# 18 heads with a column of ones in V, one float32 product that turns and folds a head's result, divisions on VectorE, and a new order of the plan

## The chip, the cores and the metric

The kernel runs on one core of one Trainium2 chip. The metric is the device time of one execution in microseconds (us), as the median of the runs shown. Engines are called as the profile calls them: PE is TensorE (PEld its weight loads), DVE is VectorE, ACT is ScalarE, POOL is GpSimd, SP issues the transfers.

## The reference: what is computed

Pooled attention over 4 batches of 8 heads, 1152 keys of 64 numbers each, queries averaged in pairs (576 of them), then a token mixer and a channel mixer. All inputs and the output are float32 (the mixers' weights arrive as float64).

```python
q_pool = q.reshape(B, H, S // 2, 2, D).mean(axis=3)          # B, H, S, D = 4, 8, 1152, 64
scores = scale * np.matmul(q_pool, k.transpose(0, 1, 3, 2))
scores = scores - np.max(scores, axis=-1, keepdims=True)
attn = np.exp(scores)
attn = attn / (np.sum(attn, axis=-1, keepdims=True) + 1e-09)
x = np.matmul(attn, v)                                       # then heads side by side: (4, 576, 512)
xt = x.transpose(0, 2, 1)
u = x + (np.maximum(xt @ w_tok1, 0.0) @ w_tok2).transpose(0, 2, 1)
out = u + np.maximum(u @ w_ch1, 0.0) @ w_ch2
```

## The kernel before

**Precision.** A float32r product on PE uses 12-bit significands. So each operand is cut into a high and a low part, and a product is the sum of three: high by high, low by high, high by low. The name of a low part ends in "l" (`pl`, `kl`, `ql`), that of a high one in "h".

**A head.** There are 32 heads, one after another (`main`). A head has 9 steps of two units; a unit is 128 keys by 288 queries. For each unit PE makes the scores in two products (line 746). ACT takes the exponential of a step twice, once in float32 (`pf`, line 756) and once rounded (`ph`, line 759). POOL, or DVE when the plan finds that sooner, subtracts the two (`pl`, line 763, through the helper `both`). Then PE multiplies `ph` and `pl` by V (line 787): the stationary operand `vv` holds V's high part in 64 columns and V's low part in the other 64, so the result `o` has 128 rows, two halves that belong together, by 288 queries. ACT copies `o` to SBUF (`ot`, line 792). The maximum that softmax needs is taken ahead of time from a second set of scores (line 681 on PE, line 683 on DVE), which pass through a ring of three PSUM banks (`r`).

**Denominators, two ways.** Ordinary heads: DVE adds up the exponentials over the keys with six reductions a head (line 769, `sum`), and five float32 products with a column of ones turn these sums into columns (line 821). Heads in the list `IN_PV` (0, 1, 2, 3 and 31): a column of V's low part is overwritten with ones (line 607), so one row of `o` is the denominator; the column that was overwritten is kept in `v0` and gets 18 products of its own, with one column of weights (line 787, `o<-ph,v`).

**Finish of a head** (`finish`). PE transposes `ot` in five pieces (line 811), into two ring banks. ACT copies the half that belongs to V's low part to SBUF (line 825), DVE adds the other half (line 827, `xx`), ACT adds epsilon to the denominators (lines 831 and 834), DVE takes reciprocals (line 837), and ACT multiplies (line 847, five pieces) into `u`.

**What else runs beside the heads.** Preparing keys, queries and V; the token mixer after every fourth head (lines 862 to 905); the token mixer's weights during the first heads. After the last head comes the channel mixer (lines 992 to 1034), for which DVE and ACT convert the weights.

**What sets the order.** Every piece of work is a step with an engine, a cost and a due time (table `DUE`, in ninths of a head). `Plan.run` walks through the time that the costs give and puts the step that is ready and due first on its engine. The result is one fixed order for each engine; on the chip an engine waits at an instruction until what it needs is there, and everything queued behind waits too.

Of the kernel before, what the change touches and what calls it, by code (L numbers as in the profile page):

```python
# [21 lines left out]
# Nanoseconds from the end of one instruction to the start of one that needs its result.  # L22
# [9 lines left out]
# When steps are due, in units of a ninth of a head, each from where its block of the plan is.  # L32
DUE = {
    "scores": -1.4,
    "p_lo": -0.03,
    "sum": -2.8,
    "pv": 1.7,
    "o": -59.42,
# [9 lines left out]
    "w_tok": -27.15,
    "w_tok_each": 7.4,
    "sum_each": 1.24,  # L50
    "pv_lo": 0.38,
    "lo_first": -0.95,
    "max_first": -139.89,
    "max_second": 10.21,
    "scores_each": -10.71,
    "p_hi": 0.24,
    "pv_one": 1.32,
    "finish_each": -23.16,
    "den_sum": -2.06,
    "x_lo": -12.52,  # L60
    "x": -1.32,
    "den": -3.43,
    "rd": -14.97,
    "u": 18.05,
    "u_each": 2.58,
    "max_of": 7.18,
    "max_row": -11.67,
    "max_first_each": 1.65,
    "q_pool": 0.33,
    "q_turn": 2.75,  # L70
    "k_each": 1.45,
    "k_hi": -3.15,
    "k_lo": 1.39,
    "q_hi": -16.83,
    "q_lo": -1.68,
    "load_kq": -56.14,
    "load_v": -170.26,
    "v_lo": -6.48,
    "load_w_tok": 80.01,
    "mix_x_lo": 3.25,  # L80
    "mix_1": 3.17,
    "mix_t": 2.06,
    "mix_2": 2.42,
    "mix_u": -23.61,
    "w_ch": 286.69,
    "w_ch_each": -5.88,
    "ut_0": -43.79,
    "ut_1": -73.8,
    "stay": 1.17,
# [3 lines left out]
class Buf:  # L93
    """A buffer out of a pool of like ones; which one it is, is settled with the order."""
# [5 lines left out]
class Step:  # L100
    """Instructions that one engine runs in one go, with what they take and when they should run."""
# [136 lines left out]
def kernel(  # L238
# [60 lines left out]
    def words(w):  # L299
        return w.bitcast(U32)  # L300
# [21 lines left out]
    def mm(n):  # L322
        return 3 + n / 2.4
# [807 lines left out]
```

## Time and profile before

| | |
|---|---|
| median of 3 runs | 993.49 us (992.21 to 997.94) |
| span of the profiled execution, first to last instruction | 992.4 us |
| the profiled execution's own time apart from its span | not given; the span lies within the runs |
| heads 0 to 3 | up to 118 us |
| heads 4 to 31 | 118 to 667 us |
| channel mixer | 667 to 992 us |

The borders are the copies of a head's second `ot` half on ACT. A row of the grouped view gives, after the bar, the busy time of the whole group in us and the mean length of one instruction in ns. The length of a PE product runs from its start to the modelled end of its result, and products overlap; the distance between the starts of two neighbours is what one takes of the engine.

### The profile page before, as it was taken

What the parts mean: (1) busy time and instruction counts of PE and PEld (TensorE: products, weight loads), DVE (VectorE), ACT (ScalarE), POOL (GpSimd) and SP (SyncE); (2) the same over time, 40 slices, a digit from 0 to 9 for tenths busy, and PEclk for the clock granted to TensorE, in tenths of its full rate; (3) what the DMA queues carried; (4) which work ended last, traced back from release to release, by engine and by line L of the source; (5) the groups of instructions that cost most, each with busy time, mean ns of one, the idle gap of its engine ahead of it and who ended that gap; (6) DMA issues with size and microseconds to landing.
All of it is one profiled execution on the core that took longest, in us unless ns stands there. A gap on an engine that the chain in (4) does not pass through costs nothing. (4 is left out here: it accounts for less than half of the span.)

```text
span 992.4 us, 15724 instructions
## 1 busy us (share of the span) xinstructions
PE 936.7 (94%) x5588; PEld 832.1 (84%) x5588; DVE 766.8 (77%) x1238; ACT 586.2 (59%) x1299; POOL 436.7 (44%) x355
## 2 busy tenths in 40 slices
PE   9989988989999899999999999999999999999998
PEld 4768887878888888888888888889999999999997
DVE  5799999999999999999999999998876212121211
ACT  1678878877886887787788788875343111111110
POOL 0354577776777787777677777520000000000000
PEclk9999989999999999999999999999999999999999
DMA  4876526435545363452742542213441101000001
GB/s 110 219 185 161 139 66 146 111 80 132 116 112 126 79 155 80 103 132 66 160 114 67 131 92 67 73 56 107 136 126 45 64 1 33 1 32 1 8 26 32
DMA packets 89846, 91.54 MB, mean 92 GB/s; under 512 B 43884, under 2 KB 68840, under 8 KB 89768
## 3 DMA queue, kind: packets, MB, share of 16 engines
q1 hardware_dynamic: 89768, 90.54, 37.4%
q8 instruction: 44, 0.72, 0.3%
q14 instruction: 34, 0.28, 0.1%
HBM read 43.25 MB, written 4.72 MB: 48 GB/s over the span
## 5 line engine op out<-in xcount | busy, mean ns | idle before, releaser
L763 POOL TENSOR_TENSOR pl<-pf,ph 128x576 fp32r<-128x576 f32 x234 | 338.8, 1456 | 154.1 <-ACT ph L759 93.8
L769 DVE TENSOR_REDUCE sum<-pf 128x96 f32<-128x864 f32 x162 | 283.2, 1749 | 0.1
L756 ACT ACTIVATE pf<-s 128x576 f32<-128x576 f32 x288 | 187.5, 654 | 76.1 <-PE s L746 63.9
L683 DVE TENSOR_REDUCE mx<-r 128x1 f32<-128x384 f32 x384 | 197.7, 549 | 9.8 <-PE r L681 8.4
L759 ACT ACTIVATE ph<-s 128x576 fp32r<-128x576 f32 x288 | 188.5, 657 | 4.2 <-PE o L787 3.3
L1000 DVE SCALAR_TENSOR_TENSOR h<-r,h 128x384 fp32r<-128x384 f32 x72 | 40.1, 557 | 170.7 <-ACT h L998 170.4
L681 PE MATMUL r<-kk,qq 128*128 128x384 f32 x372 | 143.7, 398 | 27.1 <-DVE mx L683 15.2
L746 PE MATMUL s<-qq,kk 128*128 128x288 f32 x574 | 168.2, 305 | 0.8 <-ACT ph L759 0.8
L746 PE MATMUL s<-q,k 65*128 65x288 f32 (+1 forms) x576 | 166.7, 302 | 0.0
L998 ACT ACTIVATE h<-r 128x384 fp32r<-128x384 f32 x72 | 35.4, 491 | 199.9 <-PE r L992 199.9
L787 PE MATMUL o<-pl,vv 128*128 128x288 f32 x576 | 144.5, 306 | 0.0
L787 PE MATMUL o<-ph,vv 128*128 128x288 f32 x576 | 144.4, 308 | 0.0
L1020 PE MATMUL s<-w,h 128*128 128x512 f32 x504 | 131.4, 394 | 0.0
L681 PEld LDWEIGHTS r<-kk,qq 128*128 128x128 f32 x372 | 70.6, 193 | 56.6 <-DVE mx L683 32.6
L746 PEld LDWEIGHTS s<-qq,kk 128*128 128x128 f32 x574 | 111.7, 195 | 3.5 <-ACT ph L759 2.4
L746 PEld LDWEIGHTS s<-q,k 65*128 65x128 f32 (+1 forms) x576 | 111.9, 194 | 0.6 <-issue 0.6
L992 PE MATMUL r<-big,w 128*128 128x384 f32 x576 | 108.7, 337 | 0.0
L1020 PEld LDWEIGHTS s<-w,h 128*128 128x128 f32 x504 | 93.3, 188 | 16.3
L992 PEld LDWEIGHTS r<-big,w 128*128 128x128 f32 x576 | 101.9, 188 | 3.7
L787 PEld LDWEIGHTS o<-pl,vv 128*128 128x128 f32 x576 | 101.3, 193 | 2.7 <-DVE pl L763 0.3
L787 PEld LDWEIGHTS o<-ph,vv 128*128 128x128 f32 x576 | 101.7, 193 | 1.4 <-ACT ot L792 0.3
L847 ACT ACTIVATE u<-xx,rd 128x64 f32<-128x64 f32 (+1 forms) x160 | 51.1, 346 | 7.4 <-DVE xx L827 4.0
(127 smaller groups left out, 1276.2 us busy)
## 6 DMA issues: line engine op xcount, KB each, us to landing
raw<-in_moe_w_ch_dram SPq DMA_DIRECT2D x24, 512.0 KB, 3.6
kk<-kh SPq DMA_DIRECT2D x32, 288.0 KB, 6.6
qq<-qh SPq DMA_DIRECT2D x64, 144.0 KB, 4.2
kk<-kl SPq DMA_DIRECT2D x32, 288.0 KB, 4.2
vn<-in_v_dram SPq DMA_DIRECT2D x32, 288.0 KB, 5.1
k<-kk SPq DMA_DIRECT2D x31, 288.0 KB, 3.4
kn<-in_k_dram SPq DMA_DIRECT2D x30, 288.0 KB, 5.1
qn<-in_q_dram SPq DMA_DIRECT2D x32, 256.0 KB, 6.1
```

The source lines that it names most:

```text
L681: step(PE, mm(SP3), lambda ps=ps, w=w, x=x: te.matmul(at(ps)[:, 0:SP3], w, x, start=True, stop=True), t, read, [ps], [ps])
L683: step(DVE, dve(SP3), lambda ps=ps, m=m: ve.tensor_reduce(m, at(ps)[:, 0:SP3], axis=AX.X, op=ALU.max), t + due["max_of"], [ps], [key])
L746: te.matmul(at(st)[:, i, 0:HF], w[:, c * P:(c + 1) * P], x[:, fq * HF:(fq + 1) * HF], start=(n == 0), stop=(n == len(terms) - 1))
L756: step(ACT, act_ps(2 * HF), lambda pf=pf, st=st: sc.activation(pf, at(st)[:, :, 0:HF], AF.Exp, scale=ESC), t, [(st, 0), (st, 1)], [("pf", s)])
L759: step(ACT, act_ps(2 * HF), lambda ph=ph, st=st: sc.activation(at(ph), at(st)[:, :, 0:HF], AF.Exp, scale=ESC), t + due["p_hi"], [(st, 0), ...
L763: both(2 * HF, lambda e, pf=pf, ph=ph, pl=pl: e.tensor_sub(at(pl), pf, f(at(ph))), t + due["p_lo"], [("pf", s), ph], [pl], [pl])
L769: step(DVE, dve(NK * HF // CUT), lambda fq=fq, cs=cs: ve.tensor_reduce(SUM[:, fq, cs], PF[:, fq * NK:(fq + 1) * NK, cs].rearrange("p c x - ...
L787: lambda o=o, x=x, w=w, m=m, i=i, c=c, new=new, end=end: te.matmul(at(o)[0:m], w[:, c], at(x)[:, i], start=new, stop=end),
L847: step(ACT, 240, lambda c=c, r=r, dst=dst: sc.mul(dst, x[r, c], rd[r, c]), t + due["u"] + due["u_each"] * c, [("x", i2, c // 4), ("rd", i2 ...
L992: te.matmul(at(ps)[:, 0:GT], w[:, c], x[:, c], start=(c == 0 and n == 0), stop=(c == NC4 - 1 and n == 2))
L1000: step(DVE, dve(GT), lambda: ve.scalar_tensor_tensor(out=at(h)[:, 1], in0=at(ps)[:, 0:GT], scalar=0.0, in1=f(at(h))[:, 0], op0=ALU.max, op ...
L1020: te.matmul(at(ps), a[:, x * P:(x + 1) * P], w, start=(fi == 0 and m == 0), stop=(fi == NF - 1 and m == 2))
```

## The change

- `IN_PV` grows from 5 heads to 18: heads 0 to 3 and all odd heads from 5 on. Thirteen heads lose the six DVE reductions and the five products with ones, and gain 18 products with one weight column each, and on POOL the copy and the overwriting of one column of `vv`.
- `finish` is rewritten for all heads. Five float32 products of `ot` (stationary) with a constant matrix `fold` (two identity matrices on top of each other, and for `IN_PV` heads a column that picks out the denominator) transpose and add the two halves in one go, into one ring bank. DVE adds epsilon, takes reciprocals, and multiplies straight out of PSUM into `u`, in two instructions. ACT has no part in it any more; the tiles `lo` and `xx` are gone.
- The costs that the plan uses for PE products, for the reductions and for some small steps are other numbers, and nearly all due times are. So every engine's order changes, and the plan gives other steps to DVE: 101 of the 288 subtractions `pl` (54 before), 12 of the 32 low parts of V (none before), 22 of the 48 poolings of queries (5 before); 4 of the 24 conversions' last subtractions of channel weights move from DVE to POOL.

```diff
-    IN_PV = (0, 1, 2, 3, 31)
+    IN_PV = (0, 1, 2, 3, *range(5, 32, 2))
+    FOLDS = 114
...
     def mm(n):
-        return 3 + n / 2.4
+        return 8 + n * 0.4367
...
-    "u": 18.05,
-    "u_each": 2.58,
+    "u": 18.75,
+    "u_each": 75.19,
...
+    for x in FOLD:
+        ve.tensor_add(x[:, 0:D], ident[:, 0:D], ident[:, D:2 * D])
+        ve.tensor_copy(x[:, D:D + 1], ident[:, D:D + 1])
+    ve.tensor_copy(FOLD[1][:, 0:1], ident[:, 0:1])
...
-                    step(DVE, dve(NK * HF // CUT), lambda fq=fq, cs=cs: ve.tensor_reduce(
+                    step(DVE, 65 + 1.83 * NK * HF // CUT, lambda fq=fq, cs=cs: ve.tensor_reduce(
...
     def finish(h, t):
-            step(PE, n * TURN, turn, t + k * due["finish_each"], [("ot", i2, 0), ("ot", i2, 1)], [(ps, 0)], [ps])
-                    step(PE, 214, lambda ps=ps, c=c: te.matmul(
-                        at(ps)[:, P + c:P + c + 1], sums[:, qc(c)], ones,
-            step(ACT, act_ps(n * D), lambda y=turned, r=r, c2=c2: sc.copy(
-                lo[r, c2, lo0:], y(D + lo0, P)), t + k * due["finish_each"] + due["x_lo"], keys, [("lo", pv, k)])
-            step(DVE, dve(n * D), lambda y=turned, r=r, c2=c2: ve.tensor_add(
-                x[r, c2], y(0, D), lo[r, c2]), t + k * due["finish_each"] + due["x"], [*keys, ("lo", pv, k)],
-            step(ACT, 240, lambda c=c, r=r, dst=dst: sc.mul(dst, x[r, c], rd[r, c]),
+        for c in range(NQ):
+            step(PE, FOLDS, lambda c=c: te.matmul(
+                turned()[:, c, 0:n], ot[:, qc(c)], fold[:, 0:n], start=True, stop=True),
+                t + due["finish_each"] * (c > 3), [("ot", i2, 0), ("ot", i2, 1)], [(ps, 0, c)],
+                [ps] if c == 0 else [])
+        if not pv:
+            for c in range(NQ):
+                step(PE, 112, lambda c=c: te.matmul(
+                    turned()[:, c, D:D + 1], sums[:, qc(c)], ones,
+        step(DVE, 70, lambda: ve.tensor_scalar_add(den, turned()[:, :, D:D + 1], EPS),
+             t + due["den"], keys, [("den", i2)])
+        step(DVE, 95, lambda: ve.reciprocal(rd, den), t + due["rd"], [("den", i2)], [("rd", i2)])
+        step(DVE, dve(4 * D), lambda: ve.tensor_mul(
+            u[:, c0:c0 + 4, col], turned()[:, 0:4, 0:D], rd[:, 0:4].to_broadcast([P, 4, D])),
+            t + due["u"], [*keys, ("rd", i2)], [*[("u", b, c, hh) for c in range(4)], *stage])
+        step(DVE, 260, lambda: ve.tensor_mul(
+            u[r, 8, col], turned()[r, 4, 0:D], rd[r, 4].to_broadcast([REM, D])),
+            t + due["u"] + due["u_each"], [*keys, ("rd", i2)], [("u8", b // 2, hh), *stage])
```

In the orders below `r_80`, `r_81` and `r_82` are the three ring banks. **DVE, in the middle of the attention, before.** The sums of every head (L769) stand between the maxima (L683); a finish (`xx`, `rd`) is a row here and there, and this stretch looks the same in every head.

```order
L763 TENSOR_TENSOR pl_160<-pf,ph_152 128x576
L683 TENSOR_REDUCE mx_123<-r_81 128x1
L769 TENSOR_REDUCE sum<-pf 128x96
L827 TENSOR_TENSOR xx_130<-r_80,lo_128 64x64
L837 RECIPROCAL rd_134<-den_132 128x5
L644 TENSOR_REDUCE mh<-mx_123 128x4
L557 TENSOR_TENSOR kl<-r_82,kh 128x384
L648 TENSOR_REDUCE mh<-rm 128x1
L683 TENSOR_REDUCE mx_124<-r_81 128x1
L769 TENSOR_REDUCE sum<-pf 128x96
```

The same place after, in an odd head, which has no sums:

```order
L832 TENSOR_SCALAR den_130<-r_82 128x5
L693 TENSOR_REDUCE mx_126<-r_81 128x1
L834 RECIPROCAL rd_132<-den_130 128x5
L597 TENSOR_TENSOR ql_119<-r_80,qh_117 128x192
L548 TENSOR_TENSOR qp<-qn 64x128
L839 TENSOR_TENSOR u_66<-r_82,rd_132 128x4x64
L693 TENSOR_REDUCE mx_126<-r_81 128x1
L842 TENSOR_TENSOR u_66<-r_82,rd_132 64x64
L773 TENSOR_TENSOR pl_161<-pf,ph_156 128x576
L567 TENSOR_TENSOR kl<-r_81,kh 128x384
L693 TENSOR_REDUCE mx_126<-r_81 128x1
L693 TENSOR_REDUCE mx_126<-r_82 128x1
```

The sums have left this stretch; subtractions `pl` and poolings `qp` have come in, and the finish is four rows instead of three.

**DVE a head later, where the sums of an even head stand.** Here the finish of the odd head before it is written so that its denominators are read from bank `r_82` (a row L832 with `den_131<-r_82`, eleven rows above the ones shown) and its two products stand far below:

```order
L693 TENSOR_REDUCE mx_125<-r_81 128x1
L693 TENSOR_REDUCE mx_125<-r_80 128x1
L780 TENSOR_REDUCE sum<-pf 128x96
L693 TENSOR_REDUCE mx_125<-r_81 128x1
L693 TENSOR_REDUCE mx_125<-r_80 128x1
L839 TENSOR_TENSOR u_66<-r_82,rd_133 128x4x64
L693 TENSOR_REDUCE mx_125<-r_81 128x1
L693 TENSOR_REDUCE mx_125<-r_80 128x1
L773 TENSOR_TENSOR pl_162<-pf,ph_154 128x576
L693 TENSOR_REDUCE mx_125<-r_81 128x1
L693 TENSOR_REDUCE mx_125<-r_80 128x1
L842 TENSOR_TENSOR u_66<-r_82,rd_133 64x64
```

Between `den_131` and the last of these rows stand five sums and twelve maxima, and all the maxima behind the first of the sums take turns on `r_80` and `r_81` alone. Before, a finish read a bank once and let it go:

```order
L683 TENSOR_REDUCE mx_123<-r_82 128x1
L769 TENSOR_REDUCE sum<-pf 128x96
L827 TENSOR_TENSOR xx_131<-r_80,lo_128 128x256
L905 TENSOR_TENSOR u_65<-r_82,u_65 64x256
L683 TENSOR_REDUCE mx_123<-r_81 128x1
L683 TENSOR_REDUCE mx_123<-r_80 128x1
L683 TENSOR_REDUCE mx_123<-r_82 128x1
```

What moved is the time for which a finish keeps a bank: from one row to more than a dozen.

**PE, at the finish of an ordinary (even) head, before:**

```order
L811 MATMUL r_81<-ident,ot_105 128x128
L787 MATMUL o<-ph_152,vv_120 128x288 x2
L787 MATMUL o<-pl_160,vv_120 128x288 x2
L787 MATMUL o<-ph_153,vv_120 128x288
L821 MATMUL r_81<-ones,sum 128x1 x2
L681 MATMUL r_82<-kk_92,qq_97 128x384
L821 MATMUL r_81<-ones,sum 128x1
L681 MATMUL r_80<-kk_92,qq_97 128x384
L821 MATMUL r_81<-ones,sum 128x1 x2
```

and after, with the products of the following odd head's kept column (`o<-ph,v`):

```order
L820 MATMUL r_82<-fold_109,ot_105 128x64
L827 MATMUL r_82<-ones,sum 128x1 x5
L820 MATMUL r_82<-fold_109,ot_105 128x64 x4
L691 MATMUL r_81<-kk_92,qq_97 128x384
L580 MATMUL r_80<-ident,qp 128x128
L580 MATMUL r_80<-ident,qp 128x64
L756 MATMUL s_78<-qq_96,kk_91 128x288
L756 MATMUL s_78<-q_99,k_94 128x288
L756 MATMUL s_78<-qq_96,kk_91 128x288
L756 MATMUL s_78<-q_99,k_94 128x288
L798 MATMUL o<-ph_158,v_124 1x288
L691 MATMUL r_81<-kk_92,qq_97 128x384
```

The transposes have become products with `fold`, the five products with ones stand in one block among them, and products that yield one row (`1x288`) have come in.

## Rows read from the trace of the kernel before

**Rows 1.** The page, its first part (busy us, share of the span, instructions of each engine) and its second (the span in 40 slices of 24.8 us, each digit the busy share in tenths; PEclk is the granted clock of PE in tenths).

```profile
PE 936.7 (94%) x5588; PEld 832.1 (84%) x5588; DVE 766.8 (77%) x1238; ACT 586.2 (59%) x1299; POOL 436.7 (44%) x355
PE   9989988989999899999999999999999999999998
DVE  5799999999999999999999999998876212121211
ACT  1678878877886887787788788875343111111110
POOL 0354577776777787777677777520000000000000
PEclk9999989999999999999999999999999999999999
```

**Rows 2.** Busy time of each engine in three stretches: heads 0 to 3, heads 4 to 31, the channel mixer. Columns: stretch and its length in us, then busy us of PE, PEld, DVE, ACT and POOL with the number of instructions, the mean granted clock of PE, the share of the DMA engines and GB/s.

```profile
0.00:118.00 118.00, 108.76 (x569) 84.17 (x570) 97.90 (x205) 75.72 (x174) 45.42 (x49) 0.99 0.67 161
118.00:667.00 549.00, 507.53 (x3356) 457.31 (x3356) 541.96 (x798) 436.70 (x975) 390.52 (x305) 0.98 0.45 104
667.00:992.40 325.40, 320.44 (x1667) 290.62 (x1665) 126.91 (x237) 73.80 (x152) 0.73 (x1) 1.00 0.15 48
```

**Rows 3.** DVE in order of time, in the middle of the attention: start us, length us, what, and how many alike.

```profile
410.39 1.01 DVE L683 TENSOR_REDUCE mx<-r 128x1 f32<-128x384 f32 x2
411.32 1.77 DVE L769 TENSOR_REDUCE sum<-pf 128x96 f32<-128x864 f32 x1
413.00 1.02 DVE L683 TENSOR_REDUCE mx<-r 128x1 f32<-128x384 f32 x2
413.92 1.74 DVE L769 TENSOR_REDUCE sum<-pf 128x96 f32<-128x864 f32 x1
416.97 0.75 DVE L763 TENSOR_TENSOR pl<-pf,ph 128x576 fp32r<-128x576 f32 x1
```

**Rows 4.** PE in order of time in the same head, with the idle time before an instruction where there was some.

```profile
403.04 0.34 PE L681 MATMUL r<-kk,qq 128*128 128x384 f32 x1
403.21 0.29 PE L787 MATMUL o<-pl,vv 128*128 128x288 f32 x1
403.35 0.30 PE L746 MATMUL s<-qq,kk 128*128 128x288 f32 x1
403.48 0.29 PE L746 MATMUL s<-q,k 65*128 65x288 f32 x1
403.62 0.30 PE L746 MATMUL s<-qq,kk 128*128 128x288 f32 x1
403.75 0.30 PE L746 MATMUL s<-q,k 65*128 65x288 f32 x1
403.88 0.61 PE L811 MATMUL r<-ident,ot 128*128 128x128 f32 x4
404.30 0.44 PE L681 MATMUL r<-kk,qq 128*128 128x384 f32 x1
...
404.98 0.28 PE L895 MATMUL r<-t1h,w2l 128*128 128x256 f32 x1
405.10 0.28 PE L895 MATMUL r<-t1l,w2h 128*128 128x256 f32 x1
...
416.97 0.72 PE L821 MATMUL r<-ones,sum 128*128 128x1 f32 x6
417.56 0.52 PE L549 MATMUL r<-ident,kn 128*128 128x128 f32 x3
```

**Rows 5.** Groups of instructions by line and shape: count, busy us of the group, mean ns of one, idle time before them and what ended it.

```profile
L769 DVE TENSOR_REDUCE sum<-pf 128x96 f32<-128x864 f32 x162 | 283.2, 1749 | 0.1
L763 POOL TENSOR_TENSOR pl<-pf,ph 128x576 fp32r<-128x576 f32 x234 | 338.8, 1456 | 154.1 <-ACT ph L759 93.8 <-PE o L787 20.9 <-PE r L681 11.4
L763 DVE TENSOR_TENSOR pl<-pf,ph 128x576 fp32r<-128x576 f32 x54 | 50.8, 945 | 4.3 <-ACT ph L759 2.1 <-PE o L787 1.2 <-PE r L877 0.9
L603 POOL TENSOR_TENSOR vv<-vn,vv 128x576 fp32r<-128x576 f32 x32 | 46.2, 1442 | 10.2 <-ACT vv L600 5.0 <-PE s L746 4.7 <-PE r L681 0.4
L538 DVE TENSOR_TENSOR qp<-qn 128x256 f32<-128x256 f32 x5 | 2.2, 455 | 0.0
L827 DVE TENSOR_TENSOR xx<-r,lo 128x256 f32<-128x256 f32 x32 | 13.2, 411 | 0.1
L827 DVE TENSOR_TENSOR xx<-r,lo 64x64 f32<-64x64 f32 x32 | 7.3, 228 | 1.9 <-ACT den L834 0.5 <-ACT den L831 0.4
L837 DVE RECIPROCAL rd<-den 128x5 f32<-128x5 f32 x32 | 6.0, 186 | 0.6
L847 ACT ACTIVATE u<-xx,rd 128x64 f32<-128x64 f32 x128 | 40.1, 346 | 4.6 <-DVE xx L827 4.0
L787 PE MATMUL o<-ph,v 128*1 128x288 f32 x90 | 21.1, 304 | 0.0
L821 PE MATMUL r<-ones,sum 128*128 128x1 f32 x270 | 34.2, 233 | 1.1 <-DVE sum L769 1.1
```

**Rows 6.** The waits, who waited for whom: us in total, times, longest us.

```profile
ACT pf L756 <- PE s L746: 63.9, 95, 4.6
PEld r L681 <- DVE mx L683: 34.6, 85, 1.7
PE r L681 <- DVE mx L683: 15.6, 41, 1.4
DVE mx L683 <- PE r L681: 8.4, 15, 1.0
```

**Rows 7.** The chain of work that ended last, two of its pieces in the channel mixer: start us, length us, engine, tile, line, products in the piece. Between two pieces lie the nine products of line 1020, 512 columns each.

```profile
694.27 2.10 PE r L992 x12
698.46 2.12 PE r L992 x12
```

More of the change, by code (lines that the diff above doesn't have):

```diff
@@ L34 @@
     "scores": -1.4,
[L35 to L38, printed above, removed]
+    "p_lo": 0.02,
+    "sum": -2.82,
+    "pv": 1.78,
+    "o": -107.46,
     "finish": 5.54,
-    "max": -23.13,
+    "max": -22.72,
     "max_each": 0.53,
     "prep": -32.49,
-    "v": 6.36,
-    "stack": 11.96,
-    "stack_2": 12.76,
+    "v": 9.58,
+    "stack": 29.51,
+    "stack_2": 96.51,
     "mix": 9.83,
     "mix_x": 6.03,
[L48 to L54, printed above, removed]
-    "scores_each": -10.71,
[L56 to L63, printed above, removed]
-    "u": 18.05,
-    "u_each": 2.58,
[L66 to L70, printed above, removed]
-    "k_each": 1.45,
[L72 to L80, printed above, removed]
-    "mix_1": 3.17,
[L82 to L89, printed above, removed]
+    "w_tok": -27.04,
+    "w_tok_each": 7.34,
+    "sum_each": 1.2,
+    "pv_lo": 0.54,
+    "lo_first": 7.78,
+    "max_first": -120.52,
+    "max_second": 37.69,
+    "scores_each": -10.71,
+    "p_hi": 0.84,
+    "pv_one": -0.04,
+    "finish_each": -14.96,
+    "den_sum": -47.39,
+    "x_lo": 5.05,
+    "x": -54.79,
+    "den": -45.22,
+    "rd": -27.39,
+    "u": 18.75,
+    "u_each": 75.19,
+    "max_of": 7.22,
+    "max_row": -32.02,
+    "max_first_each": -127.47,
+    "q_pool": -3.78,
+    "q_turn": 1.79,
+    "k_each": 1.45,
+    "k_hi": -42.28,
+    "k_lo": 1.7,
+    "q_hi": -79.72,
+    "q_lo": 70.53,
+    "load_kq": -48.02,
+    "load_v": -163.1,
+    "v_lo": -10.5,
+    "load_w_tok": 117.45,
+    "mix_x_lo": 3.96,
+    "mix_1": 3.17,
+    "mix_t": 2.11,
+    "mix_2": 2.45,
+    "mix_u": -79.91,
+    "w_ch": 235.24,
+    "w_ch_each": -64.39,
+    "ut_0": -4.75,
+    "ut_1": -50.96,
+    "stay": 0.78,
 }
@@ L316, in pool_, with both @@
         return 150 + 2.1 * n
-    def both(n, fn, *args):
+    def both(n, fn, *args, on=None):
+        if on == POOL:
+            return step(POOL, pool_(n), lambda: fn(po), *args)
+        if on == DVE:
+            return step(DVE, dve(n), lambda: fn(ve), *args, shared=True)
         return step(POOL, pool_(n), fn, *args, other=(DVE, dve(n)))
     def mm(n):
-        return 3 + n / 2.4
+        return 8 + n * 0.4367
     TURN = 109
@@ L800, in finish @@
         pv = h in IN_PV
[L801 removed]
+        ot, den, rd, fold = OT[i2], DEN[i2], RD[i2], FOLD[pv]
         sums = SUM.rearrange("p f x -> p (f x)")
[L803 to L836 removed]
@@ L837, in finish, with turned @@
-        step(DVE, 100, lambda: ve.reciprocal(rd, den), t + due["rd"],
-             [("den", i2, y) for y in range(2)], [("rd", i2)])
+        n, ps = D + int(pv), Buf("r")
+        def turned():
+            return at(ps)[:, 0:NQ * (D + 1)].rearrange("p (c x) -> p c x", c=NQ)
+        for c in range(NQ):
[3 more added lines that the diff above has]
+                [ps] if c == 0 else [])
@@ new lines, in finish @@
+        keys = [(ps, 0, c) for c in range(NQ)]
+        if not pv:
+            for c in range(NQ):
+                step(PE, 112, lambda c=c: te.matmul(
+                    turned()[:, c, D:D + 1], sums[:, qc(c)], ones,
+                    start=True, stop=True), t + due["den_sum"],
+                     [*[("sum", y, z) for y in range(2) for z in range(CUT)], keys[0]], [(ps, 1, c)])
+            keys += [(ps, 1, c) for c in range(NQ)]
+        step(DVE, 70, lambda: ve.tensor_scalar_add(den, turned()[:, :, D:D + 1], EPS),
+             t + due["den"], keys, [("den", i2)])
@@ L841, in finish @@
         stage = [("stage",)] if b >= 2 else []
-        for c in range(NQ):
-            r = rows(c)
-            dst, key = (
-                (u[r, c0 + c, col], ("u", b, c, hh)) if c < 4
-                else (u[r, 8, col], ("u8", b // 2, hh)))
-            step(ACT, 240, lambda c=c, r=r, dst=dst: sc.mul(dst, x[r, c], rd[r, c]),
-                 t + due["u"] + due["u_each"] * c, [("x", i2, c // 4), ("rd", i2)], [key, *stage])
+        r = rows(4)
+        step(DVE, dve(4 * D), lambda: ve.tensor_mul(
[4 more added lines that the diff above has]
+            t + due["u"] + due["u_each"], [*keys, ("rd", i2)], [("u8", b // 2, hh), *stage])
     def token_mix(b, i, t):
```

32 lines of the change are left out of this document (4 added, 28 removed).

## The prediction

> **What bounds the kernel now.** The page comes first. In its 40 slices DVE shows a 9 from the third slice to the twenty-seventh, and PE nines and eights throughout [rows 1]. So two engines claim the attention, and the page does not settle which. The view by stretches does. In heads 4 to 31, 549 us, DVE is busy for 541.96 us, 98.7% [rows 2]. PE's 507.53 us there are lengths that overlap: four products of 288 columns start 0.53 us apart in all, 403.35 to 403.88, 0.133 us each, though each is 0.30 us long [rows 4]. What PE really needs must be counted. A product takes 0.133 us of it with 288 columns, 0.175 with 384 (403.04 to 403.21; and 12 of these with nine of 512 columns fill 4.19 us in the last stage [rows 4, 7]), 0.12 with 256, a transpose 0.105 (0.42 us for four) [rows 4]. A float32 product with ones shows as two instructions (270 for 135 products [rows 5]), and six of these take 0.59 us, so it takes 0.197 us [rows 4]. The 28 heads hold 2016 products of 288 columns (268 us), 378 of 384 for the maxima (66), 336 transposes of keys, queries and results (35), 135 products with ones (27), 406 of 256 columns for the token mixer (49) and 18 for kept columns (2): 447 us, 81% of the stretch. PE and ACT therefore wait for DVE, directly and in a circle: the maxima's products for a bank (34.6 + 15.6 us), the exponentials for scores that are queued behind them (63.9 us), while DVE waits for maxima only 8.4 us in all [rows 6]. In heads 0 to 3 DVE is busy 97.9 of 118 us, in the channel mixer PE is at 320 of 325 us [rows 2].
>
> A page speaks on this reading. The Trainium skill (Trainium Kernel Development and Optimization, Performance Expectations) says that PE's matmul busy time misleads and that the busy share of weight loads is the better measure. The trace agrees: weight loads fill 457.31 of the 549 us, 83% [rows 2], near the counted 81%; by that measure PE's need below would be some 10 us higher.
>
> **Part by part, heads 4 to 31 (549 us).**
>
> *Sums leave DVE.* Thirteen heads lose six reductions. One holds DVE for 1.68 us (411.32 to 413.00 [rows 3]; its own length is 1.749 us [rows 5]): 78 x 1.68 = 131 us off DVE, on the bounding engine with 0.1 us of idle time before all of them [rows 5].
>
> *Finish on DVE.* The two additions `xx` go, 28 x (411 + 228 ns) = 18 us [rows 5]. Two products out of PSUM of the same shapes come. No row shows a multiplication with a repeated divisor; the additions are the nearest, so +18 us. Adding epsilon is like the reciprocal on 5 numbers, 186 ns [rows 5]: +5 us at most.
>
> *Work that the plan gives to DVE.* 47 more subtractions `pl`, 945 ns on average beside POOL, 0.75 us undisturbed [rows 3, 5]: +35 to +44 us, I take 44. 12 low parts of V, the same size: +11. 17 poolings at up to 455 ns [rows 5]: +5. DVE's sum: 542 - 131 - 18 + 18 + 5 + 44 + 11 + 5 = 476 us, bounds 463 to 480. POOL, at 390.5 of 549 us, loses 47 x 1456 ns and 12 x 1442 ns [rows 2, 5] and gets 13 copies and overwritings of one column, small beside that: it stays hidden as long as V is prepared well ahead; if it were not, the products of `ph` and V would wait, and the scores queued behind them on PE.
>
> *PE.* 65 products with ones go: -13 us. 234 products for kept columns come. A row shows them as long as other 288-column products (304 ns [rows 5]), though only one weight column is loaded, so 0.133 us each: +31 us. The 140 products with `fold` replace 140 transposes. A float32 product with 64 moving columns stands in no row. It is bounded below by the transpose, 0.105 us, and above by twice the product with ones, 0.39 us; the nearest row is the product with ones, which also loads 128 float32 weight columns twice, so I take 0.197 us: +13 us, ends 0 and +40. PE's sum: 447 - 13 + 31 + 13 = 478 us, bounds 465 to 505. To this come stretches at half clock: the mean granted clock of 0.98 [rows 2] stands for some 22 us at 1.2 instead of 2.4 GHz, 11 us lost; as PE idles less, I count 5. PE's need is 483 us.
>
> *ACT* loses its part of the finish (line 847 alone is 40.1 us [rows 5]); it was at 437 of 549 us [rows 2] and goes lower. It gains nothing by itself.
>
> *What is late next.* PE needs 483 us and DVE 476: the bound moves from one engine to two that are nearly equal. Both run fixed orders, and each waits for the other: maxima's products for banks, reductions for products. Before, DVE reached 98.7% because no other engine needed more than 81%. That cannot be expected of two equal ones, and no row shows what can. I bound it by 100% of PE's need (483 us, a gain of 66) and 90% (537 us, a gain of 12), and take 95%: 508 us, a gain of 41.
>
> *Waits that are added.* The products with ones stand in one block before four of the five `fold` products, so PE stops there until the last of six sums is done, with the next scores queued behind it; before, the block was split by maxima, but it waited for the same sums. On DVE the finish's products wait for `fold` products on PE, with maxima and subtractions queued behind. Its bank is kept until the second product, in every odd head across five sums and twelve maxima (5 x 1.68 + 12 x 0.465 us, nearly 14 us [rows 3]), and maxima have two banks meanwhile. All of this I count in the 95%.
>
> *Elsewhere.* Heads 0 to 3 had ones in V already and still have; only their finish and the order change: 0, give or take 4 us. The channel mixer's PE work is the same and follows without a gap [rows 7]; DVE's conversions there are covered (127 of 325 us [rows 2]): 0.
>
> **Sum.** The profiled execution has no time of its own beside its span of 992.4 us; the median of the runs is 993.49, 1 us more. 992.4 - 41 = 951, and with that 1 us, 952 us.
>
> **Rivals.**
>
> *The float32 product is dearer.* At 0.39 us a `fold` product, PE needs 447 - 13 + 31 + 40 + 5 = 510 us and is the only bound, DVE being at 476; at 97% that is 526 us, a gain of 23: 970 us. Against it stands that the product with ones shows two instructions and 0.197 us [rows 4, 5], for it that one moving column says nothing of 64. The Trainium skill (FP8 and Floating Point Precision, TensorE Precision Notes) says that a true float32 product makes four passes through the array; the trace shows two instructions each, so by that rule 0.39 us would be right only if the passes were not already inside those two.
>
> *The gain stays behind in the ring.* If the kept bank makes every pair of heads wait 2.9 us more, 14 pairs lose 41 us and the time is that of before, 993. For it: waits for a bank are already the longest of PE [rows 6]. Against it: a maximum on two banks only has to keep pace with the mixture on DVE, where a 1.68 us sum stands behind every second maximum in that stretch.
>
> *Slower: PE was the bound all along.* Should PE's 92% be its real load, its added work (31 + 13 - 13 us) would all lie on the path, and what DVE saves would be saved beside it: 993 + 31 = 1024 us. This decides from the point where a 288-column product takes 0.178 us of PE in place of 0.133: then the 447 us counted before, with 2016 x 0.045 us more and the 11 us at half clock, fill the 549 us. The starts in order of time speak against it [rows 4], and DVE's own 98.7% [rows 2].
>
> *Better.* The two engines interlock well: above 98%, under 934 us.
>
> **How the numbers follow.** Chances: forecast 0.66, with 934 to 970 as its own range; dearer float32 product 0.10 (965 to 984); ring keeps the gain 0.07; slower 0.06; better than 934 0.11. The likeliest gives 952. The range runs from 928, the full use of PE's need, to 984, which takes in the dearer product and the 90% bound; it leaves out the two last bad cases and a part of the better one, some 0.18. Beyond 0.5% (5 us, about what a measurement of this kernel can tell from no change): faster 0.66 + 0.10 + 0.11 = 0.87, same 0.07, slower 0.06.
>
> **What would show it.** In heads 4 to 31: 84 sums in all instead of 162; DVE's busy time near 476 us, in a stretch near 508; distances of 0.133 us for the one-row products and about 0.2 us for a `fold` product; idle time on both PE and DVE of a few per cent, with waits for banks on PE. The prediction is wrong if DVE is still busy over 97%, if a `fold` product takes 0.3 us or more, if waits on the ring grow by tens of us, or if heads 0 to 3 or the channel mixer change by more than 5 us.

## The result and the profile after

| | before | after |
|---|---|---|
| median | 993.68 us (992.21 to 997.94, 4 runs) | 965.12 us (963.99 to 965.73, 4 runs) |
| span of the profiled execution | 992.4 us | 963.5 us |
| heads 0 to 3 | 118.1 us | 125.5 us |
| heads 4 to 31 | 549.1 us | 511.3 us |
| channel mixer | 325.2 us | 326.7 us |

The ratio is 0.9716, 95% interval 0.9691 to 0.9742: faster by 28.6 us, where the forecast had 41. The forecast was 952 us with a range of 928 to 984. The stretches are cut at the copy of the second `ot` half of heads 3 and 31 on ACT, as before.

The page of the kernel after, its first part and three rows of the slices (24.1 us each):

```profile
PE 934.6 (97%) x5852; PEld 845.2 (88%) x5852; DVE 703.5 (73%) x1268; ACT 514.3 (53%) x1038; POOL 353.4 (37%) x309
...
PE   9979899999999999999999999999999999999997
...
DVE  6799999899899899989998989988882212121211
...
PEclk7789999999999999999999999999999999999999
```

The view by stretches, columns as in [rows 2]:

```profile
0.00:125.50 125.50, 110.34 (x581) 86.79 (x582) 105.19 (x215) 69.80 (x147) 43.51 (x48) 0.86 0.68 156
125.50:636.80 511.30, 503.53 (x3605) 467.75 (x3604) 473.35 (x821) 372.22 (x750) 303.08 (x256) 0.99 0.48 110
```

DVE's row of the page, all nines before from the third slice on [rows 1], now has eights. In heads 4 to 31 DVE is busy for 473.35 of 511.3 us, 92.6%, where it was 98.7% [rows 2], and weight loads rose from 83% to 91% of the stretch: the two engines are now nearly equally full.

Groups by line and shape, columns as in [rows 5]:

```profile
L780 DVE TENSOR_REDUCE sum<-pf 128x96 f32<-128x864 f32 x84 | 147.4, 1763 | 0.9 <-ACT pf L766 0.8
...
L773 DVE TENSOR_TENSOR pl<-pf,ph 128x576 fp32r<-128x576 f32 x101 | 93.4, 930 | 2.1 <-ACT ph L769 1.5
...
L839 DVE TENSOR_TENSOR u<-r,rd 128x256 f32<-128x256 f32 x32 | 13.3, 415 | 0.1
...
L842 DVE TENSOR_TENSOR u<-r,rd 64x64 f32<-64x64 f32 x32 | 7.1, 227 | 0.8
...
L832 DVE TENSOR_SCALAR den<-r 128x5 f32<-128x5 f32 x32 | 5.2, 162 | 18.0 <-PE r L820 18.0
```

The 84 sums are there, and the two multiplications with a repeated divisor take 415 and 227 ns, as the additions did that they were priced by (411 and 228 [rows 5]). New is the idle time of 18.0 us before `den`, when DVE waits for the `fold` products.

PE in order of time, columns as in [rows 4], at the finish of an ordinary head (first five rows) and of a head with ones:

```profile
405.36 0.43 PE L798 MATMUL o<-ph,v 128*1 128x288 f32 x2
405.63 0.49 PE L580 MATMUL r<-ident,qp 128*128 128x128 f32 x3
...
406.86 1.23 PE L827 MATMUL r<-ones,sum 128*128 128x1 f32 x10
407.95 1.08 PE L820 MATMUL r<-fold,ot 128*128 128x64 f32 x8
408.84 0.42 PE L691 MATMUL r<-kk,qq 128*128 128x384 f32 x1
...
419.40 1.22 PE L820 MATMUL r<-fold,ot 128*128 128x65 f32 x10
420.44 1.32 PE L873 MATMUL r<-big,big 128*128 128x256 f32 x9
```

A float32 product again shows as two instructions. Five `fold` products take 419.40 to 420.44, 0.208 us each, and four take 407.95 to 408.84, 0.22 each; five products with ones take 406.86 to 407.95, 0.218 each. So 64 moving columns cost no more than one. Two kept-column products fill 0.27 us, 0.135 each.

The waits, as in [rows 6]:

```profile
ACT pf L766 <- PE s L756: 80.3, 96, 4.3
...
DVE mx L693 <- PE r L691: 14.5, 21, 4.0
...
PEld r L691 <- DVE mx L693: 12.1, 19, 2.3
...
PE r L691 <- DVE mx L693: 6.8, 10, 2.1
```

PE's waits for maxima fell from 34.6 + 15.6 us [rows 6] to 12.1 + 6.8, and DVE's for maxima's products rose from 8.4 to 14.5. Counted from the starts of PE's products, as the prediction does, PE's need in heads 4 to 31 is some 476 us, 93% of the stretch; it was some 443 before when the starts are added up one by one (447 in the prediction, from groups). Both are estimates, good to some 5 us.

**Heads 0 to 3** grew by 7.4 us: head 1 from 26.7 to 31.2 us and head 2 from 19.6 to 22.5. DVE (four rows), POOL (two) and PE (the last) in order of time at the border of heads 0 and 1:

```profile
51.80 6.12 DVE L352 TENSOR_SCALAR w<-w 128x256 f32<-128x256 f32 x2 [0.62 <-ACT w L351]
57.84 0.48 DVE L355 TENSOR_SCALAR w<-w 128x256 uint32<-128x256 uint32 x2
...
59.58 0.15 DVE L832 TENSOR_SCALAR den<-r 128x5 f32<-128x5 f32 x1
...
60.43 0.23 DVE L842 TENSOR_TENSOR u<-r,rd 64x64 f32<-64x64 f32 x1
...
51.73 1.20 POOL L548 TENSOR_TENSOR qp<-qn 128x256 f32<-128x256 f32 x2 [3.31 <-DMA qn<-in_q_dram]
...
53.62 4.14 POOL L773 TENSOR_TENSOR pl<-pf,ph 128x576 fp32r<-128x576 f32 x3
...
60.71 0.44 PE L691 MATMUL r<-kk,qq 128*128 128x384 f32 x1 [3.38 <-DVE u L842]
```

Two small operations of the weights' conversion, 0.48 us for two of their kind one row below, take 6.12 us, until POOL's unbroken work ends at 57.76. The finish of head 0 is queued behind them on DVE, keeps its bank, and PE stands still for 3.38 us. The kernel before has the same kind of stall in the same place, DVE first, then PE:

```profile
53.97 4.29 DVE L355 SCALAR_TENSOR_TENSOR w<-u,w 128x256 uint32<-128x256 uint32 x2
58.29 0.23 DVE L827 TENSOR_TENSOR xx<-r,lo 64x64 f32<-64x64 f32 x1
...
59.78 0.42 DVE L827 TENSOR_TENSOR xx<-r,lo 128x256 f32<-128x256 f32 x1
...
54.31 0.71 PE L811 MATMUL r<-ident,ot 128*128 128x128 f32 x5
...
59.03 0.47 PE L570 MATMUL r<-ident,qp 128*128 128x128 f32 x1 [2.33 <-DVE qp L538]
```

There it lasted 4.29 us, with two subtractions in POOL's row instead of three. The finish kept its two banks across it, from the transposes at 54.31 to the additions `xx`, and PE stood still for 2.33 us, waiting for a pooling that was queued behind the stall. So the change made a stall longer that was there already.

The view by stretches has a granted clock of 0.86 in heads 0 to 3, where it was 0.99 [rows 2]. In the kernel after PE ran at 1.2 GHz, half of its 2.4 GHz, from 10 to 30 us. The stretch from 10 to 20 us, first of the kernel after and then of s1_no_kept (an experiment below), columns as in [rows 2]:

```profile
10.00:20.00 10.00, 10.00 (x21) 4.68 (x19) 4.86 (x12) 1.58 (x5) 0.00 (x0) 0.50 0.73 155
10.00:20.00 10.00, 10.00 (x22) 4.93 (x21) 4.67 (x10) 1.58 (x5) 0.00 (x0) 1.00 0.52 106
```

That is not what made heads 0 to 3 longer: s1_no_kept, at full clock there, takes 125.8 us for them, and b1_ones_old_order, at 0.50 from 10 to 30 us like the kernel after, takes 116.3.

### The profile page after: what moved, and what is told of

Same layout as the page of the kernel before. It is cut to its first block, busy times and chain, and to the rows that moved or that the text cites. A ratio compares the mean times of both kernels' runs of the same rounds, so it can differ in the third digit from the quotient of the medians.

```text
span 963.5 us, 15874 instructions
## 1 busy us (share of the span) xinstructions
PE 934.6 (97%) x5852; PEld 845.2 (88%) x5852; DVE 703.5 (73%) x1268; ACT 514.3 (53%) x1038; POOL 353.4 (37%) x309
## 4 chain that ended last, share of the span: by engine, by line
PE 77%; DVE 17%; ACT 3%; DMA 2%; issue 1%; DVEq 0%; SPq 0%; ACTq 0%
PE r L988 16%; PE o L798 14%; PE s L1016 12%; PE s L756 10%; PE r L691 7%; DVE mx L693 6%; DVE pl L773 3%; PE r L820 3%; PE r L891 3%; DVE sum L780 3%; PE o L1016 3%; PE r L873 2%; PE r L827 2%; DMA kk<-kl 1%; PE r L559 1%
## 5 line engine op out<-in xcount | busy, mean ns | idle before, releaser
L773 POOL TENSOR_TENSOR pl<-pf,ph 128x576 fp32r<-128x576 f32 x187 | 267.7, 1452 | 155.2 <-ACT ph L769 107.7
L693 DVE TENSOR_REDUCE mx<-r 128x1 f32<-128x384 f32 x384 | 198.6, 553 | 17.3 <-PE r L691 14.5
L769 ACT ACTIVATE ph<-s 128x576 fp32r<-128x576 f32 x288 | 187.9, 659 | 0.0
L780 DVE TENSOR_REDUCE sum<-pf 128x96 f32<-128x864 f32 x84 | 147.4, 1763 | 0.9 <-ACT pf L766 0.8
L691 PE MATMUL r<-kk,qq 128*128 128x384 f32 x372 | 131.7, 369 | 14.1 <-DVE mx L693 6.8
L798 PE MATMUL o<-pl,vv 128*128 128x288 f32 x576 | 139.4, 299 | 0.3 <-DVE pl L773 0.3
L773 DVE TENSOR_TENSOR pl<-pf,ph 128x576 fp32r<-128x576 f32 x101 | 93.4, 930 | 2.1 <-ACT ph L769 1.5
```

Of the source, the lines that this page charges most:

```text
L691: step(PE, mm(SP3), lambda ps=ps, w=w, x=x: te.matmul(at(ps)[:, 0:SP3], w, x, start=True, stop=True), t, read, [ps], [ps])
L693: step(DVE, dve(SP3), lambda ps=ps, m=m: ve.tensor_reduce(m, at(ps)[:, 0:SP3], axis=AX.X, op=ALU.max), t + due["max_of"], [ps], [key])
L769: step(ACT, act_ps(2 * HF), lambda ph=ph, st=st: sc.activation(at(ph), at(st)[:, :, 0:HF], AF.Exp, scale=ESC), t + due["p_hi"], [(st, 0), ...
L773: both(2 * HF, lambda e, pf=pf, ph=ph, pl=pl: e.tensor_sub(at(pl), pf, f(at(ph))), t + due["p_lo"], [("pf", s), ph], [pl], [pl], on=LO[s])
L780: step(DVE, 65 + 1.83 * NK * HF // CUT, lambda fq=fq, cs=cs: ve.tensor_reduce(SUM[:, fq, cs], PF[:, fq * NK:(fq + 1) * NK, cs].rearrange(" ...
L798: lambda o=o, x=x, w=w, m=m, i=i, c=c, new=new, end=end: te.matmul(at(o)[0:m], w[:, c], at(x)[:, i], start=new, stop=end),
```

## The experiments

Eleven kernels are versions of the two, one is a small measurement by itself. "28 heads" is heads 4 to 31.

| label | median us | ratio to before (interval) | heads 0 to 3 | 28 heads |
|---|---|---|---|---|
| (after) | 965.12 | 0.9716 (0.9691 to 0.9742) | 125.5 | 511.3 |
| s1_no_kept | 961.75 | 0.9678 (0.9625 to 0.9732) | 125.8 | 510.9 |
| s2_short_sums | 963.76 | 0.9705 (0.9667 to 0.9742) | 126.7 | 507.6 |
| s3_both | 955.20 | 0.9617 (0.9574 to 0.9660) | 125.4 | 499.5 |
| s4_before_short | 913.82 | 0.9193 (0.9151 to 0.9235) | 117.6 | 472.9 |
| b2_short13 | 961.56 | 0.9671 (0.9632 to 0.9710) | 115.2 | 517.0 |
| b1_ones_old_order | 975.46 | 0.9827 (0.9761 to 0.9894) | 116.3 | 528.4 |
| e1_before_ones | 1003.67 | 1.0096 (1.0071 to 1.0121) | 117.1 | 558.2 |
| e2_after_five | 1066.64 | 1.0726 (1.0668 to 1.0784) | 126.7 | 615.0 |
| e4_old_costs | 1002.71 | 1.0102 (1.0066 to 1.0137) | 121.4 | 551.2 |
| e3_u_together | 980.44 | 0.9870 (0.9825 to 0.9914) | 125.7 | 519.9 |
| e5_u_inplace | 966.47 | 0.9726 (0.9710 to 0.9742) | 124.8 | 512.4 |

### What bounds heads 4 to 31, before and after

**s4_before_short**, the kernel before with all its sums cut short, in its own order:

```diff
-                        PF[:, fq * NK:(fq + 1) * NK, cs].rearrange("p c x -> p x c"),
+                        PF[:, fq * NK:fq * NK + 1, cs].rearrange("p c x -> p x c"),
```

> The kernel before in the same order, with its 162 reductions over one chunk of keys instead of nine (denominators of 27 heads are wrong): some 245 us off DVE. Theory (DVE bound alone before and PE needed 447 us of the 549): heads 4 to 31 fall to 460 to 490 us, 905 to 935 us in all. Rival (PE was the bound all along at 92% busy): under 20 us faster, 973 us or more.

The stretch view of this kernel, heads 4 to 31:

```profile
117.60:590.50 472.90, 462.83 (x3358) 447.86 (x3357) 330.58 (x798) 424.41 (x975) 385.53 (x305) 0.99 0.52 121
```

The expectation held. The 28 heads lose 76 us, with PE's work as before. So DVE was the bound before, and PE's need there is at most 473 us: "PE was the bound all along" falls.

**s1_no_kept**, **s2_short_sums** and **s3_both** take load from the kernel after in its own order: the kept-column products (PE), most of each sum (DVE), and both.

```diff
# s1_no_kept and s3_both
-                         lambda o=o, x=x, w=w, m=m, i=i, c=c, new=new, end=end: te.matmul(
+                         lambda o=o, x=x, w=w, m=m, i=i, c=c, new=new, end=end: m == 1 or te.matmul(
# s2_short_sums and s3_both
-                        PF[:, fq * NK:(fq + 1) * NK, cs].rearrange("p c x -> p x c"),
+                        PF[:, fq * NK:fq * NK + 1, cs].rearrange("p c x -> p x c"),
```

> The changed kernel in the same order on every engine, without the 324 products of the kept column (the result lacks the low part of one column of V). It takes 43 us of work off PE (324 x 0.133), 34 us of it in heads 4 to 31, and leaves DVE, ACT and POOL as they are. Theory (PE and DVE are needed nearly equally, and each waits for the other): 8 to 20 us faster than the changed kernel, 945 to 957 us. Rival A (PE alone bounds, as its 98% busy share says): the whole 34 to 43 us, 922 to 931 us. Rival B (DVE still bounds alone): at most 4 us, 961 us or more.

> The changed kernel in the same order, with its 84 reductions over one chunk of keys instead of nine (denominators of 14 heads are wrong). It takes some 84 x 1.5 = 126 us off DVE and nothing off the other engines. Theory: the stretch falls to what PE needs and little more, 483 us instead of 511, so 15 to 30 us faster, 935 to 950 us. Rival A (PE alone bounds): under 5 us faster, 960 us or more. Rival B (DVE alone bounds): 60 us or more, under 905 us.

> Both cuts at once, same order: PE needs some 449 us in heads 4 to 31 and DVE some 350. Theory: the sum of more than the two alone, 50 to 65 us faster, 900 to 915 us, since each alone leaves the other engine in the way. Rival (waits in the fixed order, not the engines' loads, hold the time): under 30 us, 935 us or more.

The stretch views, heads 4 to 31, of s1_no_kept:

```profile
125.80:636.80 511.00, 495.87 (x3354) 462.08 (x3353) 471.60 (x820) 371.92 (x750) 302.91 (x256) 0.97 0.48 110
```

of s2_short_sums:

```profile
126.70:634.30 507.60, 501.68 (x3605) 467.24 (x3605) 360.33 (x821) 371.92 (x750) 304.82 (x256) 0.99 0.48 111
```

and of s3_both:

```profile
125.40:624.90 499.50, 484.25 (x3353) 450.56 (x3353) 357.37 (x820) 370.39 (x749) 304.94 (x256) 0.99 0.49 112
```

The waits of DVE in s2_short_sums:

```profile
DVE mx L693 <- PE r L691: 74.6, 61, 8.3
DVE den L832 <- PE r L820: 36.3, 27, 2.4
```

Against the kernel after, the medians are 3.4, 1.4 and 9.9 us lower. All three expectations missed (8 to 20, 15 to 30 and 50 to 65 us), and s3 gave the number of its rival: waits in the fixed order, not the engines' loads, hold the time. By their numbers s1 rules out PE as the only bound, and s2 DVE. In the 28 heads of the profiled executions, taking some 34 us of products from PE (252 x 0.133) gives nothing (511.3 to 510.9), and taking 113 us from DVE gives 3.7. The first of these is weaker than it looks: the execution is the slowest of s1's four (955.84 to 965.21 us), and its granted clock there is 0.97 instead of 0.99, which takes back some 10 us. With short sums DVE only waits more, 74.6 us for maxima's products where it was 14.5. With both gone the heads take 499.5 us, 12 less, though PE needs only some 442 us of them (476 - 34) and DVE 357. So most of what lies between PE's need and the time belongs to the written order: s4_before_short has about the same PE need (some 443 us) and takes 472.9 us in the order of before. That beside it the two loads hold each other rests on the step of 12 us alone; it is argued, not shown. What an order fitted to s3's loads would take was not tried.

### How much of it is the order

**b2_short13** leaves the kernel before as it is, in its order, but cuts the sums short in the thirteen heads that the change relieves; **b1_ones_old_order** does in these heads what the change does to them (ones in V, kept column, no sums, no products with ones), in the same places of the same order, with the old finish. In b1 the reciprocals stay where they stood, so that in those heads four of five chunks of queries are divided by an earlier head's denominators.

```diff
# b2_short13
+    ONES = (0, 1, 2, 3, *range(5, 32, 2))
...
-                        PF[:, fq * NK:(fq + 1) * NK, cs].rearrange("p c x -> p x c"),
+                        PF[:, fq * NK:fq * NK + (1 if h in ONES else NK), cs].rearrange("p c x -> p x c"),
# b1_ones_old_order
+            if h in ONES and h not in IN_PV:
+                po.tensor_copy(V0[h % 2], vv[:, :, D:D + 1])
+                po.memset(f(vv)[:, :, D:D + 1], 1.0)
...
+                        if also:
+                            te.matmul(at(o)[0:1], V0[i2][:, c], at(x)[:, i], start=False, stop=False)
```

> The kernel before in its own order, with the reductions of the same 13 heads over one chunk of keys instead of nine (their denominators are wrong): some 118 us off DVE, and nothing added anywhere. Theory: heads 4 to 31 fall to 470 to 495 us, 912 to 940 us in all; the distance to the run with the ones in the old order is the price of 234 products more and 65 less on PE, at most 18 us. Rival (half of the sums is not enough, since the other half still bounds its heads): over 955 us.

> The kernel before, with its order left as it is (costs, due times and plan untouched), and the 18 heads put in where they stand: in 13 heads the reductions and the products with ones are left out of their places, each product of ph with V is followed at once by the product of the kept column, the column of ones is written right behind V's low part, and ACT adds epsilon to the denominators out of the turned result. Finish, copies and divisions stay on ACT as before. Theory (DVE alone held the old order and PE had some 100 us of idle time to give): heads 4 to 31 fall from 549 to 490 to 510 us, 932 to 955 us in all, faster than the changed kernel. Rival (what brought the gain is the fitted order, since the same list planned anew gave 1004): over 975 us.

The stretch views, heads 4 to 31, of b2_short13:

```profile
115.20:632.20 517.00, 485.94 (x3358) 455.11 (x3358) 444.18 (x798) 429.92 (x976) 389.67 (x305) 0.98 0.48 110
```

and of b1_ones_old_order:

```profile
116.30:644.70 528.40, 499.66 (x3462) 451.49 (x3461) 424.83 (x720) 435.44 (x988) 392.90 (x331) 1.00 0.47 108
```

b2 missed my expectation of 55 us or more: it is 33 us faster than before, and its rival (over 955 us, since the other half of the sums still bounds its heads) came out. In the old order the relief is local. Odd heads, without long sums, fall from 19.1 to 16.8 us on average; even heads stay at 20.1, and DVE's freed time is not filled with their work. b1 costs 14 us more than b2: the products added on PE less those removed, priced at 31 - 13 = 18 in the prediction, here on the path; the clock, 0.98 in b2 and 1.00 in b1, does not make that difference, since it goes the other way. b1 missed as well: 932 to 955 us expected, 975.46 measured, just at its rival's border (over 975 us, the gain comes from the fitted order). From b1 to the kernel after, 10 us: the finish in one bank, and the new order with the DVE work that it moves; which of the two, no run separates. b1's four runs lie between 972 and 987 us, so these steps of 14 and 10 us are each uncertain by some 6 us. b2's time is no longer than that of the kernel after: the sums' removal alone is worth the whole gain, and what the change adds to PE and takes back by finish and order cancel, as far as these runs can tell.

**e1_before_ones**, **e2_after_five** and **e4_old_costs** let the plan make a new order: the kernel before with the list of 18, the kernel after with the list of 5, and the kernel after with the two old costs.

```diff
# e1_before_ones (e2_after_five is the reverse, in the kernel after)
-    IN_PV = (0, 1, 2, 3, 31)
+    IN_PV = (0, 1, 2, 3, *range(5, 32, 2))
# e4_old_costs
-        return 8 + n * 0.4367
+        return 3 + n / 2.4
...
-                    step(DVE, 65 + 1.83 * NK * HF // CUT, lambda fq=fq, cs=cs: ve.tensor_reduce(
+                    step(DVE, dve(NK * HF // CUT), lambda fq=fq, cs=cs: ve.tensor_reduce(
```

> The kernel before with the list of 18 heads alone; finish, costs and due times stay those of before. Theory (the sums that leave DVE are the gain, 131 us off the bounding engine, and PE's 31 - 13 us more fill its idle time): 15 to 45 us faster than before, 950 to 980 us, less than the changed kernel gives if the due times were fitted to it. Rival (the gain is from the rewritten finish and the new order): within 5 us of before.

> The changed kernel with the old list of 5 heads: the new finish, costs and due times without the ones. Theory: DVE carries 162 sums again and bounds, 985 to 1000 us, the time of before. Rival (finish and order bring the gain): 965 to 975 us.

> The changed kernel with the old costs of PE products and of the reductions (3 + n / 2.4 and 65 + 1.042 n) in the plan, so that only the order differs. If the plan's costs matter with two engines near their limits: 8 to 25 us slower than the changed kernel, 973 to 990 us. If any order does about as well: within 6 us, 959 to 971 us.

All three missed both what was expected and its rival. e1 (950 to 980 us expected) has the relief and the old finish, b1's work, and it is 1% slower than before; its 28 heads take 30 us more than b1's. e4 (8 to 25 us slower expected) computes what the kernel after does and is 38 us slower; e2 (985 to 1000 us expected) takes 104 us more than the kernel after in its 28 heads, a part of it at half clock (granted clock 0.90 there, 0.99 in the kernel after). The due times are good for one set of steps and costs, and any change that makes the plan decide anew costs tens of us. An edit through the plan therefore says little about the edit; edits in place (s1 to s4, b1, b2) do.

### The kept bank

**e3_u_together** sets the due time between the two products of a finish to 2.58 (75.19 in the kernel after) and lets the plan order anew. **e5_u_inplace** keeps the order and only puts the second product right behind the first. In e5 that product stands, in heads 8, 12, 24 and 28, ahead of the token mixer's last row of the batch before, whose last 64 queries share its rows; these come out with other values, and the amount of work is the same.

```diff
# e3_u_together
-    "u_each": 75.19,
+    "u_each": 2.58,
# e5_u_inplace
-        step(DVE, dve(4 * D), lambda: ve.tensor_mul(
-            u[:, c0:c0 + 4, col], turned()[:, 0:4, 0:D], rd[:, 0:4].to_broadcast([P, 4, D])),
+        def divide():
+            ve.tensor_mul(
+                u[:, c0:c0 + 4, col], turned()[:, 0:4, 0:D], rd[:, 0:4].to_broadcast([P, 4, D]))
+            ve.tensor_mul(
+                u[r, 8, col], turned()[r, 4, 0:D], rd[r, 4].to_broadcast([REM, D]))
+
+        step(DVE, dve(4 * D), divide,
```

> The changed kernel with the due time of the second product of a finish right behind the first (u_each 2.58 instead of 75.19), so that the ring bank is let go sooner; the plan puts other steps elsewhere too. If the kept bank costs time in every odd head: 10 to 25 us faster than the changed kernel, 940 to 955 us. If the order absorbs it: within 6 us, 959 to 971 us.

> The changed kernel, its written order kept but for one thing: the second product of a finish (weights u, the half of the head's result that the fold adds) stands right behind the first, so that the bank it writes is let go sooner and the copies of scores behind it may start earlier. Nothing is left out. Theory (the time is TensorE's count of steps plus the order's own gaps; the bank that a finish keeps costs little): within 4 us of the changed kernel, 961 to 969. Rival (the ring of banks holds back a part of the gain): 8 us faster or more, below 957, most of it in heads 4 to 31.

e3 is 15 us slower, another order made anew, and neither of its two expectations came out. The second product is the multiplication for a head's last 64 queries; it reads the bank, and does not write it as the expectation of e5 has it. e5, at 966.47 us, is within 1.4 us of the kernel after, and its 28 heads take 512.4 us, so the theory holds: the gap between the two products costs nothing that can be measured. The rest of the hold, from `den` to the first product, was not shortened.

### DVE beside POOL

**p1_port** times four kinds of DVE operation, each let go just after POOL has begun a row of 0, 1, 2 or 4 subtractions.

```python
for fn in cases:          # tensor_scalar; two SBUF tiles; PSUM and SBUF; sum
    for n in (0, 1, 2, 4):
        po.tensor_sub(a, b, e)
        for i in range(n):
            po.tensor_sub(z[i], x, y)
        fn()
```

> A small kernel that leaves out the whole computation (its outputs are zeros) and times one thing: four kinds of VectorE operation on 128 x 256 numbers (a tensor_scalar from SBUF to SBUF, a subtraction of two SBUF tiles, a subtraction of an SBUF tile from a PSUM one, a sum over an SBUF tile), each let go just after GpSimd has begun a row of 0, 1, 2 or 4 subtractions on 128 x 576 that follow each other without a gap. Theory (an operation of the first kinds waits until GpSimd's unbroken row ends, as the 6.12 us for two weight roundings in head 0 suggest): the first two kinds take about 1.4 us longer for every subtraction in the row, so over 5 us at four, and the other two kinds take the same at 0 and at 4. Rival (the two engines take turns): no kind takes over 1.5 us longer at any length of the row, or all four kinds grow alike.

DVE in order of time, with 0, 1 and 4 subtractions (first kind), 0 and 4 (second), 4 (third and fourth); then POOL at the first kind's 4:

```profile
4.21 0.28 DVE L61 TENSOR_SCALAR d<-a 128x256 f32<-128x256 f32 x1
5.33 1.47 DVE L61 TENSOR_SCALAR d<-a 128x256 f32<-128x256 f32 x1 [0.83 <-POOL a L69]
...
11.07 1.47 DVE L61 TENSOR_SCALAR d<-a 128x256 f32<-128x256 f32 x1 [1.97 <-POOL a L69]
17.22 0.43 DVE L62 TENSOR_TENSOR d<-a,b 128x256 f32<-128x256 f32 x1 [4.67 <-POOL a L69]
...
24.48 1.60 DVE L62 TENSOR_TENSOR d<-a,b 128x256 f32<-128x256 f32 x1 [1.97 <-POOL a L69]
...
37.45 0.42 DVE L63 TENSOR_TENSOR d<-bank,a 128x256 f32<-128x256 f32 x1 [2.96 <-POOL a L69]
...
50.22 0.42 DVE L64 TENSOR_REDUCE g<-a 128x1 f32<-128x256 f32 x1 [2.97 <-POOL a L69]
...
11.01 5.50 POOL L71 TENSOR_TENSOR z<-x,y 128x576 f32<-128x576 f32 x4
```

The theory falls for a single operation: the first two kinds wait out the subtraction that is running (1.47 for 0.28 us, 1.60 for 0.43) and no more, however long the row is, which is the number of the rival. The other two kinds wait for nothing (0.42 us at 0 and at 4).

## Why the prediction was right, step by step

965.12 us lies in the range and in the forecast's own part of it, 934 to 970. The bound, the relief and the prices are borne out by the runs; the 95% is borne out in its size only, and one small term, heads 0 to 3, was wrong.

- *DVE bounded heads 4 to 31.* Shown by s4_before_short.
- *DVE's new load of 476 us.* 473.35 measured. The terms hold one by one: 84 sums, the finish at 415 and 227 ns, epsilon at 162 ns, subtractions `pl` at 930 ns.
- *PE's need of 483 us.* Some 476 counted, beside 478 without half clock, and half clock almost gone (granted clock 0.99). The two prices without a row were the right ones: 0.208 to 0.22 us for a `fold` product (taken: 0.197, ends 0.105 and 0.39) and 0.135 us for a kept-column product (taken: 0.133). The rival of a dearer float32 product falls with that. The four passes of the Trainium skill (FP8 and Floating Point Precision, TensorE Precision Notes) are, if they are made, inside the two instructions.
- *95% of PE's need, 508 us.* 511.3 measured, of which the counted need is some 93%. The size was right; the reason, two engines of nearly equal need that wait for each other, is not shown. s4_before_short reaches 94% with PE alone loaded (DVE 331 of 473 us), so two equal engines are not needed for a loss of this size. Relieving one alone gives 0 to 4 us (s1, s2), relieving both 12 (s3), and PE's share then falls to 88%. What keeps the kernel from PE's need is mostly the order's own waits, which the prediction did not name. That 95% came out so near is in part luck.
- *Removal on the bounding engine.* The prediction drew 131 us off DVE and let others fill it. In the old order the 13 heads' sums are worth 33 us (b2). The time goes where the sums were and is not spread over other heads.
- *The ring keeps the gain.* Not so: PE's waits for maxima's banks fell from 50 to 19 us, and e5 shows that the second product's place costs nothing. The prediction had named waits for banks on PE as a sign of its being right; that sign did not come.
- *Heads 0 to 3: 0, give or take 4.* This term was mis-sized: +7.4 us measured, past the 5 us that the prediction gives as a sign of being wrong. It is more than half of what lies between 952 and 965; the 28 heads gave 37.8 of the 41 us, the channel mixer took 1.5 us more. The prediction counted the finish on DVE as the same length there and did not ask what is queued ahead of it. The rows show a finish behind a 6.12 us stall, PE idle for 3.38 us behind it, and PE's granted clock at 0.66 from 60 to 70 us. But the kernel before had 4.29 us, 2.33 us, and a clock of 0.93 and 0.90 from 50 to 60 and 60 to 70 us. So only the differences count: 1 us of standing still and some 2 us lost at half clock (0.34 x 10 us against 0.07 x 10 and 0.10 x 10), estimates from these numbers. That they account for most of the 4.5 us in head 1 was not tested, and head 2's 2.9 us are not explained. The loss does not come with the longer list: with the old finish and ones in 18 heads, heads 0 to 3 take 116.3 us in the order of before (b1) and 117.1 in a new one (e1). Every kernel with the new finish takes 121 to 127 us for them, whatever its order, and every one with the old finish 115 to 118; this points to the finish or its due times, which no run separates.

## What to carry to other kernels

When a change relieves the bounding engine, add up the need of the next one from the distances between its starts, and price new operations from the nearest rows; both held here. That need filled some 93% of the time here, 94% in s4 and 88% in s3, by the written order more than by how equal the engines are, so carry it over as a range and not as a number. Test single causes in place, in an order that stays written as it is: a plan that was made anew moved the time by 15 (e3) and 38 us (e4) with the same work, and hid what it was asked about. Price the first stages, where other work is queued, apart from the steady ones.

## What the runs showed of the hardware

- A float32 product of 128 weight columns with 64 or 65 moving columns takes PE 0.208 to 0.22 us, no more than one with a single moving column (0.218).
- A DVE operation that takes one SBUF tile in (tensor_scalar) or two waits out POOL's running instruction: 0.28 becomes 1.47 us, 0.43 becomes 1.60; one with an input in PSUM (0.42) and a sum (0.42) do not wait. The Trainium skill (SBUF — State Buffer, Who interferes with whom) says that the two engines share one port pair, held for a whole instruction, and that sums never contend; p1_port agrees. The kernel shows more: of the two tensor_scalar operations in the row of 6.12 us the first took 0.82 us, until a POOL instruction ended, and the second 5.38, until all that POOL had left was done; before, the two in the row of 4.29 us took 0.96 and 3.41. p1_port has one operation in a row and did not show this; why the second waits longer stays open.
- In s1, without the kept-column products, the granted clock over the 28 heads was 0.97 where the kernel after has 0.99; in s3, without the same products, it was 0.99. So it varies with the same PE work, and that less work lowers it is not shown.
